# Conversions and transposes of the late weights tied behind the additions and products written ahead of them

## The chip, the cores and the metric

The kernel runs on one core of one Trainium2 chip. The metric is the device time of one execution in microseconds (us), the median of the runs that were made; lower is better. The core has a matrix engine (TensorE, "PE" in the profile, with its weight loads as "PEld"), three elementwise engines (VectorE "DVE", ScalarE "ACT", GpSimd "POOL"), and a queue engine (SyncE, "SP") that starts the DMA transfers here. Each engine runs its instructions strictly in the order of its own queue and waits on semaphores for the others.

## What is computed

Packed attention over 8 batches, then two feed-forward blocks. The part that matters is the second half of the first block and the weights of the second:

```python
x = np.ascontiguousarray(attn_out.transpose(0, 2, 1, 3)).reshape(B * S, H * D)   # 4608 x 512

def _moe_ref(x, w_gate, w_val, w_out):          # 512 -> 1536 -> 512
    g = x @ w_gate
    silu = g * (1.0 / (1.0 + np.exp(-g)))
    val = x @ w_val
    return (silu * val @ w_out).astype(np.float32)

def _moe2_ref(x, w1, w2, w3, w_out):            # 512 -> 1024 -> 1024 -> 512
    a = x @ w1
    b = x @ w2
    h = a * b @ w3
    return (h @ w_out).astype(np.float32)
```

`w3` and the second `w_out` have nothing between them, so the kernel multiplies them once (1024 x 1024 by 1024 x 512) and uses the product as one weight. The weights arrive as 64-bit numbers and must be turned into 32-bit ones on the chip. Every large product is made of three matmuls, high part by high part, high by low and low by high, so each operand is split into `hi` and `lo`.

## The kernel before

The tokens go through the first block in four passes P of two batches each (2P and 2P + 1, the first index in names such as `u6_2`), and in each pass over twelve blocks f of 128 columns (the second index). For every batch and block, stage 1 makes two products on PE, `pg` and `pv` (12 matmuls each, L445); ACT writes `u = Silu(pg)` (L450), DVE multiplies `u` by `pv` (L454), ACT rounds it to `uh` (L96) and POOL subtracts to get `ul` (L89). After every third block, stage 3 multiplies three blocks of `uh`, `ul` by the output weights into six tiles `px` (L674, 18 matmuls each, three tiles at a time); the first of the four groups of a pass is copied to `acc` by ACT (L682), the later ones are added to it by DVE (L686). Ahead of three blocks come their `pc` products (32 matmuls each, L412), which ACT and DVE split into `ch` and `cl`. PSUM is used as four tiles in turn: a new `pg`, `pv`, `px`, `pc` or `pw` must wait until the reader of the tile's last content is done.

During the last pass (P = 3, batches 6 and 7, blocks 0 to 9) `w3_task` is called at one to four places ("slots") of each block, and each call does a piece of the weight work of the second block. The list of pieces is four tiles of `w_out2`, eight of `w3`, and the same again (c = 0 and c = 1). For each tile, `w3_conv` converts it: ACT takes the high word (Prelu, L349), DVE shifts the low word (`vx`, L350) and joins the two (`vt`, L353); then the next raw tile is loaded. A `w_out2` tile is split on ACT and POOL (`wo2h`, `wo2l`). A `w3` tile (c, r) is transposed on DVE in the next call (`w3_T`, L749, one buffer), split on ACT (`w3h`) and POOL (`w3l`, two buffers each), and in the call after that multiplied: `pw` is 12 matmuls (L766) that take `w3h` first and `w3l` from the third matmul on. For c = 0 ACT copies the result out (L770); for c = 1 DVE adds the stored half to it (`w3o`, L772); either one frees the PSUM tile.

The order of each engine's queue is not written out: a scheduler sorts the instructions by their dependencies and by priority. `behind(x, what)` adds a dependency without a semaphore: it puts x behind the instruction `pin[what]` in the order and lets nothing wait for it at run time. Inside `w3_task` the dictionary `pin` was empty, so conversions and transposes went wherever the scheduler found their inputs ready. `pin_at` remembers the latest instruction of a kind as the program is written.

Of the kernel before, what the change touches and what calls it, by code (L numbers as in the profile page):

```python
# [13 lines left out]
ALU = mybir.AluOpType  # L14
# [24 lines left out]
def packed_attention_moe_kernel(  # L39
# [24 lines left out]
    nc = tc.nc  # L64
# [29 lines left out]
    def split(hi, lo, src, on="act", sub_on="dve"):  # L94
        if on == "act":
            nc.scalar.copy(hi, src)  # L96
        else:
            nc.vector.tensor_copy(hi, src)
        sub(lo, src, hi, sub_on)
# [26 lines left out]
    def psum(name):  # L126
        ps_n[0] += 1
        return ps_at[ps_n[0] % len(ps_at)].tile([128, 2, 512], F32, tag="A", name=name)
# [9 lines left out]
    in_front, conv_rest, pin, pin_at = [True], [], {}, {}  # L138
    NO_SYNC = mybir.DependencyInfo(mybir.DependencyClass.NoSync, mybir.DependencyReason.DATA)

    def behind(x, what):
        if what in pin:
            tc.add_manual_dep(x.ins, pin[what].ins.name, NO_SYNC, reason="behind the last unit")
# [192 lines left out]
    def conv(key, t):  # L336


        name, raw = raw_t.pop(0)
        assert name == key, (name, key)  # L340
        x = vc.tile(list(t.shape), I32, tag="vx", name=f"vx_{key}")
        w = raw.bitcast(I32)
        if len(t.shape) == 3:
            w = w.rearrange("p a (n e) -> p a n e", e=2)
            low, high = w[:, :, :, 0], w[:, :, :, 1]
        else:
            w = w.rearrange("p (n e) -> p n e", e=2)
            low, high = w[:, :, 0], w[:, :, 1]
        behind(nc.scalar.activation(t, high.bitcast(F32), AF.Prelu, scale=2.0 ** -112, alpha=-2.0 ** 32), "act")  # L349
        behind(nc.vector.tensor_scalar(x, low, 29, None, op0=ALU.logical_shift_right), "dve")  # L350

        def rest():
            nc.vector.scalar_tensor_tensor(  # L353
                t.bitcast(I32), t.bitcast(I32), 3, x, op0=ALU.logical_shift_left, op1=ALU.bitwise_or)

        if in_front[0]:
            conv_rest.append(rest)
        else:
            rest()
        if not in_front[0]:  # L360
            raw_load()
# [69 lines left out]
    def stage1(b, f, gv):  # L431
        if (b, f) not in s1_at:
            s1_at[b, f] = (up0 if in_front[0] or b % 2 == 0 else up).tile(
                [128, 2, HS], F32, tag="u", name=f"u{b}_{f}", bufs=1)
        u = s1_at[b, f]
        hi, lo = C_t[b // 2, f]
        ah, al = aT_t[b]
        cols = slice(128 * gv, 128 * gv + 128)
        t = psum(f"p{'gv'[gv]}{b}_{f}")
        for Q in range(2):  # L440
            for w, x, first, last in (
                (hi, ah, Q == 0, False), (hi, al, False, False), (lo, ah, False, Q == 1),
            ):
                for hf in range(2):
                    nc.tensor.matmul(  # L445
                        t[:, hf, 0:HS], lhsT=w[:, b % 2, Q, cols], rhs=x[:, Q, hf, :],
                        start=first, stop=last,
                    )
        if gv == 0:
            x = nc.scalar.activation(u, t[:, :, 0:HS], AF.Silu)  # L450
            if not in_front[0]:
                pin_at["act"] = x
            return
        x = nc.vector.tensor_tensor(out=u, in0=u, in1=t[:, :, 0:HS], op=ALU.mult)  # L454
        if not in_front[0]:
            pin_at["dve"] = x
        P = b // 2
        if (P, f) not in u_pair:
            at = up0 if len(u_pair) % NU < NU0 else up
            u_pair[P, f] = tuple(  # L460
                at.tile([128, 2, 2, HS], F32R, tag=f"u{x}", name=f"u{x}{P}_{f}") for x in "hl")
        uh, ul = u_pair[P, f]
        split(uh[:, b % 2], ul[:, b % 2], u, sub_on="pool")
        u_t[b, f] = (uh, ul)
# [53 lines left out]
    def pa_s(u):  # L518


        kT = kT_t.pop(u)
        t = psum(f"psp{u}")
        for hq in range(4):
            for e in range(2):
                es = slice(64 * e, 64 * e + 64)
                nc.tensor.matmul(
                    t[hs[hq], e, 0:HS].rearrange("j (m p) -> j m p", m=NR // 2), lhsT=kT[es, NR // 2, hs[hq]],
                    rhs=kT[es, 0:NR // 2, hs[hq]],
                    start=True, stop=True, tile_position=(64 * e, 32 * hq))
        mx = pa.tile([128, 1], F32, tag="mx", name=f"mx{u}")  # L530
        nc.vector.reduce_max(mx, t[:, :, 0:HS], axis=AX.XY)
        nc.vector.tensor_scalar_mul(mx, mx, -scale)
        return t, mx
# [77 lines left out]
    for f in range(2):  # L611
        task(CS[f] + 0.5, c_mm, 0, f)
        task(CO[f], lambda: c_out(*C_t["later"].pop(1)))
        for gv in range(2):
            task(S1[f] + gv, stage1, 0, f, gv)
# [7 lines left out]
    with tc.manual_schedule(engines=M0):  # L623
        for s in range(last + 1):
# [8 lines left out]
            if 0 <= s - 1 < U:  # L633
                x = pa_s(s - 1)
# [25 lines left out]
    acc = {}  # L660

    CW = 2 * S // 3
# [16 lines left out]
    def stage3_out(P, g, j, t):  # L679
        if g == 0:  # L680
            o = up.tile([128, 2, CW], F32, tag=f"acc{j}", name=f"acc{P}_{j}", bufs=1)
            nc.scalar.copy(o, t[:, :, 0:CW])  # L682
            acc[j] = o
        else:
            o = acc[j]
            pin_at["acc"] = nc.vector.tensor_tensor(out=o, in0=o, in1=t[:, :, 0:CW], op=ALU.add)  # L686
        if g == NG - 1:
            for h in range(2):
                d, c = divmod(2 * j + h, 3)
                t0 = 2 * S * P + CW * c  # L690
                if j % 3 == 1:
                    nc.sync.dma_start(X2d[d, :, t0:t0 + CW], o[:, h])
                elif h == 0:
                    nc.sync.dma_start(X2d[d, :, t0:t0 + 2 * CW], o.rearrange("p h s -> p (h s)"))

    def stage3(P, g, e):
        for j in range(ND // 2 * 3 // 2 * e, ND // 2 * 3 // 2 * (e + 1)):
            t = psum(f"px{P}_{g}_{j}")
            stage3_mm(P, g, j, t, range(GF))
            stage3_out(P, g, j, t)  # L700
# [31 lines left out]
    wo2_t, w3T = {}, {}  # L732

    def w3_conv(key):
        t = vl.tile([128, 512], F32, tag="vu", name=f"vt_{key}")
        conv(key, t)
        what, *at = key.split("_")
        c = int(at[0])
        if what == "wo2":
            hi = wp.tile([128, DM], F32R, tag="wo2h", name=f"wo2h{c}", bufs=W3B)  # L740
            lo = wp.tile([128, DM], F32R, tag="wo2l", name=f"wo2l{c}", bufs=W3B)
            split(hi, lo, t, sub_on="pool")
            wo2_t[c] = (hi, lo)
        else:
            w3T[c, int(at[1])] = t

    def w3_T(new):
        t = wp.tile([128, 512], F32, tag="w3T", name=f"w3T{new}", bufs=1)
        nc.vector.transpose(out=t, in_=w3T[new])  # L749
        hi = wp.tile([128, 4, 32, 4], F32R, tag="w3h", name=f"w3h{new}")  # L750
        lo = wp.tile([128, 4, 32, 4], F32R, tag="w3l", name=f"w3l{new}")
        split(hi, lo, t.rearrange("p (r k b) -> p k b r", r=4, k=4), sub_on="pool")
        w3T[new] = tuple(x.rearrange("p k b r -> p k (b r)") for x in (hi, lo))
# [21 lines left out]
    def w3_step(new, old):  # L775
        if old is not None:
            w3_mm(old)
        if new is not None:
            w3_T(new)
# [91 lines left out]
    def w3_task(P, f, slot):  # L871

        if P < NPR - 1 or slot not in W3S[f % GF] or f > 9 or (f == 0 and slot < 3):
            return
        i = w3_at[0]
        w3_at[0] += 1
        if 0 < i <= len(w3_list) and w3_list[i - 1].startswith("w3"):
            new = tuple(int(x) for x in w3_list[i - 1].split("_")[1:])
            w3_step(new, w3_old[0])
            w3_old[0] = new  # L880
            if new[1] == NF2 - 1:
                w3_step(None, new)
                w3_old[0] = None
        if i < len(w3_list):
            w3_conv(w3_list[i])

    for n, (P, f) in enumerate(steps):
        def at(i):
# [2 lines left out]
        if P > 0:  # L891
            wo_split(P, f)
        w3_task(P, f, 0)
        if n > 1 and at(1) is not None and n < NF:
            c_mm(*at(1))
# [5 lines left out]
        if (2 * P, f) not in u_t:  # L901
            stage1(2 * P, f, 0)
            stage1(2 * P, f, 1)
# [13 lines left out]
        if at(1) is not None and at(1)[0] > 0:  # L917
            wo_load(*at(1))
        w3_task(P, f, 1)
        if pend is not None:  # L920
            stage3(*pend, 0)
        w3_task(P, f, 2)
        stage1(2 * P + 1, f, 0)
        if n == 1:
# [210 lines left out]
```

## Time and profile before

| | us |
|---|---|
| median of three runs | 1360.7 (1360.44 to 1363.02) |
| the profiled execution | 1364.69 |
| its span in the trace | 1362.6 |
| PE busy in it | 1339.7 (98%) |
| DVE, ACT, POOL busy | 656.5, 570.1, 387.8 |

The span is what the trace records from first to last instruction; 2.1 us of the profiled execution lie around it. The mean granted clock of PE is 0.996. The weight work of `w3_task` lies between 580 and 785 us. The page cuts numbers out of names (`vt_w` stands for a `w3` tile, `vt_wo` for one of `w_out2`); only the `w3T`, `w3h` and `w3l` keep theirs.

### The profile page before, as it was taken

What the parts mean: (1) busy time and instruction counts of PE and PEld (TensorE: products, weight loads), DVE (VectorE), ACT (ScalarE), POOL (GpSimd) and SP (SyncE); (2) the same over time, 40 slices, a digit from 0 to 9 for tenths busy, and PEclk for the clock granted to TensorE, in tenths of its full rate; (3) what the DMA queues carried; (4) which work ended last, traced back from release to release, by engine and by line L of the source; (5) the groups of instructions that cost most, each with busy time, mean ns of one, the idle gap of its engine ahead of it and who ended that gap; (6) DMA issues with size and microseconds to landing.
All of it is one profiled execution on the core that took longest, in us unless ns stands there. A gap on an engine that the chain in (4) does not pass through costs nothing.

```text
span 1362.6 us, 25518 instructions
## 1 busy us (share of the span) xinstructions
PE 1339.7 (98%) x10196; PEld 1241.7 (91%) x10196; DVE 656.5 (48%) x962; ACT 570.1 (42%) x940; POOL 387.8 (28%) x309
## 2 busy tenths in 40 slices
PE   7999999999999999999999999999999999999998
PEld 5678899999999999989999999999899899998997
DVE  3756877336564466462463379633423234234230
ACT  5774644244443454344554146423333333233331
POOL 0332322323322333243444237312112021121120
PEclk9999999999999999989999999999999999999999
DMA  9976766534545443244443249828448266285441
GB/s 318 341 222 206 209 197 200 168 77 125 151 131 183 115 120 125 71 134 132 151 142 111 65 166 338 311 89 254 160 142 254 91 211 215 88 254 162 142 145 47
DMA packets 186822, 230.27 MB, mean 169 GB/s; under 512 B 70736, under 2 KB 117840, under 8 KB 186704
## 3 DMA queue, kind: packets, MB, share of 16 engines
q1 hardware_dynamic: 186704, 228.64, 53.7%
q8 instruction: 81, 1.33, 0.4%
q14 instruction: 37, 0.30, 0.1%
HBM read 179.04 MB, written 49.55 MB: 168 GB/s over the span
## 4 chain that ended last, share of the span: by engine, by line
PE 81%; DVE 4%; DMA 1%; issue 1%; ACT 1%; SPq 0%; POOL 0%; DVEq 0%; ACTq 0%
PE px L674 19%; PE po L1072 14%; PE pA L1008 13%; PE pg L445 9%; PE pv L445 9%; PE pB L1008 6%; PE pw L766 3%; PE pC L1008 3%; PE pc L412 2%; DVE ws L89 1%; PE psq L209 1%; DMA wo3r<-wo3d 0%; DMA x2r<-X2d 0%; DVE x2T L836 0%; DMA X2d<-acc 0%
## 5 line engine op out<-in xcount | busy, mean ns | idle before, releaser
L89 POOL TENSOR_TENSOR ul<-u,uh 128x576 fp32r<-128x576 f32 x96 | 146.9, 1532 | 304.9 <-ACT uh L96 278.9
L1028 POOL TENSOR_TENSOR c<-s,s 128x384 f32<-128x384 f32 x48 | 49.2, 1024 | 375.7 <-ACT s L1023 375.5
L674 PE MATMUL px<-uh,woh 128*128 128x384 f32 x576 | 148.2, 338 | 0.2
L674 PE MATMUL px<-ul,woh 128*128 128x384 f32 x576 | 146.7, 335 | 0.0
L674 PE MATMUL px<-uh,wol 128*128 128x384 f32 x576 | 146.6, 335 | 0.0
L1023 ACT COPY s<-pA 128x384 f32<-128x384 f32 x144 | 69.0, 479 | 178.6 <-PE pA L1008 172.2
L454 DVE TENSOR_TENSOR u<-u,pv 128x576 f32<-128x576 f32 x96 | 72.0, 751 | 139.8 <-PE pv L445 126.3
L1072 PE MATMUL po<-wo_hi,abl 128*128 128x512 f32 x288 | 112.2, 390 | 0.0
L1072 PE MATMUL po<-wo_lo,abh 128*128 128x512 f32 x288 | 112.2, 390 | 0.0
L1072 PE MATMUL po<-wo_hi,abh 128*128 128x512 f32 x288 | 112.1, 389 | 0.0
L96 ACT CAST uh<-u 128x576 fp32r<-128x576 f32 x96 | 64.6, 673 | 110.7 <-DVE u L454 110.5
L674 PEld LDWEIGHTS px<-uh,woh 128*128 128x128 f32 x576 | 103.0, 189 | 6.4 <-issue 2.9
L686 DVE TENSOR_TENSOR acc<-acc,px 128x768 f32<-128x768 f32 x72 | 68.0, 948 | 81.5 <-PE px L674 81.1
L674 PEld LDWEIGHTS px<-ul,woh 128*128 128x128 f32 x576 | 104.4, 188 | 0.0
L674 PEld LDWEIGHTS px<-uh,wol 128*128 128x128 f32 x576 | 104.3, 188 | 0.0
L89 POOL TENSOR_TENSOR wol<-wof,woh 128x512 fp32r<-128x512 f32 x48 | 65.2, 1370 | 126.9 <-ACT woh L96 121.8
L89 DVE TENSOR_TENSOR abl<-ab,abh 128x768 fp32r<-128x768 f32 x48 | 49.2, 1025 | 105.3 <-ACT abh L96 105.2
L450 ACT ACTIVATE u<-pg 128x576 f32<-128x576 f32 x96 | 62.4, 650 | 88.3 <-PE pg L445 81.7
L445 PE MATMUL pg<-aTh,ch 128*128 128x288 f32 x384 | 84.3, 301 | 1.2 <-DVE cl L89 0.7
L445 PE MATMUL pv<-aTh,ch 128*128 128x288 f32 x384 | 82.9, 297 | 0.9 <-DVE cl L89 0.6
L445 PE MATMUL pg<-aTh,cl 128*128 128x288 f32 x384 | 82.4, 296 | 0.5 <-DVE cl L89 0.5
L445 PE MATMUL pg<-aTl,ch 128*128 128x288 f32 x384 | 82.6, 297 | 0.0
(308 smaller groups left out, 3093.6 us busy)
## 6 DMA issues: line engine op xcount, KB each, us to landing
ws<-wsd SPq DMA_DIRECT2D x245, 256.0 KB, 3.0
wf<-Wd SPq DMA_DIRECT2D x36, 512.0 KB, 6.4
wsd<-ws SPq DMA_DIRECT2D x49, 256.0 KB, 3.6
km<-in_k_dram SPq DMA_DIRECT2D x16, 576.0 KB, 7.8
wof<-wod SPq DMA_DIRECT2D x36, 256.0 KB, 2.9
x2r<-X2d SPq DMA_DIRECT2D x24, 384.0 KB, 5.2
out_dram<-o SPq DMA_DIRECT2D x36, 256.0 KB, 2.0
vm<-in_v_dram SPq DMA_DIRECT2D x16, 512.0 KB, 8.2
```

Of the source, the lines that this page charges most:

```text
L89: x = eng.tensor_tensor(out=out, in0=src, in1=hi.bitcast(F32), op=ALU.subtract)
L96: nc.scalar.copy(hi, src)
L445: nc.tensor.matmul(t[:, hf, 0:HS], lhsT=w[:, b % 2, Q, cols], rhs=x[:, Q, hf, :], start=first, stop=last,)
L450: x = nc.scalar.activation(u, t[:, :, 0:HS], AF.Silu)
L454: x = nc.vector.tensor_tensor(out=u, in0=u, in1=t[:, :, 0:HS], op=ALU.mult)
L674: nc.tensor.matmul(t[:, h, 0:CW], lhsT=w[:, 128 * d:128 * d + 128], rhs=x[:, CW * c:CW * c + CW], start=first, stop=last,)
L686: pin_at["acc"] = nc.vector.tensor_tensor(out=o, in0=o, in1=t[:, :, 0:CW], op=ALU.add)
L766: nc.tensor.matmul(t[:, 1], lhsT=a[:, kk], rhs=w, start=(i == 0), stop=(i == 11))
L1008: nc.tensor.matmul(bk[n], lhsT=w[:, hl, 128 * d:128 * d + 128], rhs=r[:, d], start=(first and d == 0 and i == 0), stop=(d == 1 and i == 2) ...
L1023: nc.scalar.copy(o, t)
L1028: on.tensor_tensor(out=r, in0=o, in1=t, op=op)
L1072: nc.tensor.matmul(t, lhsT=a[:, j, cols], rhs=w[:, f], start=first, stop=last)
```

## The change

Two places remember one more instruction: stage 1 the product of L454, and stage 3 the addition of L686, both under the key "out", so that the later written one of the two stands there. `w3_task` fills `pin` before its work and empties it after: what goes through `behind(x, "dve")` is put behind the latest product or addition written so far, and what goes through `behind(x, "act")` behind the latest Silu. That holds for `vx` on DVE and the Prelu on ACT, which called `behind` already, and for the transposes of `w3`, which are now given to it as well. `vt` follows `vx` by its data, and the splits follow the transposes. No instruction is added or removed, and nothing is computed in another way.

```diff
@@ stage1
         x = nc.vector.tensor_tensor(out=u, in0=u, in1=t[:, :, 0:HS], op=ALU.mult)
         if not in_front[0]:
-            pin_at["dve"] = x
+            pin_at["dve"] = pin_at["out"] = x
@@ stage3_out
             o = acc[j]
-            pin_at["acc"] = nc.vector.tensor_tensor(out=o, in0=o, in1=t[:, :, 0:CW], op=ALU.add)
+            pin_at["acc"] = pin_at["out"] = nc.vector.tensor_tensor(out=o, in0=o, in1=t[:, :, 0:CW], op=ALU.add)
@@ w3_T
-        nc.vector.transpose(out=t, in_=w3T[new])
+        behind(nc.vector.transpose(out=t, in_=w3T[new]), "dve")
@@ w3_task
         w3_at[0] += 1
+        pin.update(dve=pin_at["out"], act=pin_at["act"])
         if 0 < i <= len(w3_list) and w3_list[i - 1].startswith("w3"):
...
         if i < len(w3_list):
             w3_conv(w3_list[i])
+        pin.clear()
```

Three places of DVE's queue show what moves. The order of PE's matmuls stays as it was, but for one `px` matmul that changes places with one of the first `pw`. The first place is the end of pass 2 and the first block of pass 3, where the last group of `px` of pass 2 is added to `acc2_0` to `acc2_2`. Before:

```order
L454 TENSOR_TENSOR u6_0_7013<-u6_0_7013,pv6_0_7028 128x576
L353 SCALAR_TENSOR_TENSOR vt_wo2_3_7432<-vt_wo2_3_7432,vx_wo2_3_7433 128x512
L350 TENSOR_SCALAR vx_w3_0_0_7478<-raw_w3_0_0_7282 128x512
L350 TENSOR_SCALAR vx_w3_0_1_7498<-raw_w3_0_1_7337 128x512
L353 SCALAR_TENSOR_TENSOR vt_w3_0_0_7477<-vt_w3_0_0_7477,vx_w3_0_0_7478 128x512
L749 STREAM_TRANSPOSE w3T(0, 0)_7491<-vt_w3_0_0_7477 128x512
L686 TENSOR_TENSOR acc2_0_5726<-acc2_0_5726,px2_3_0_7050 128x768
L353 SCALAR_TENSOR_TENSOR vt_w3_0_1_7497<-vt_w3_0_1_7497,vx_w3_0_1_7498 128x512
L749 STREAM_TRANSPOSE w3T(0, 1)_7560<-vt_w3_0_1_7497 128x512
L686 TENSOR_TENSOR acc2_1_5747<-acc2_1_5747,px2_3_1_7071 128x768
L350 TENSOR_SCALAR vx_w3_0_2_7567<-raw_w3_0_2_7382 128x512
L353 SCALAR_TENSOR_TENSOR vt_w3_0_2_7566<-vt_w3_0_2_7566,vx_w3_0_2_7567 128x512
L749 STREAM_TRANSPOSE w3T(0, 2)_7655<-vt_w3_0_2_7566 128x512
L686 TENSOR_TENSOR acc2_2_5768<-acc2_2_5768,px2_3_2_7093 128x768
L454 TENSOR_TENSOR u7_0_7114<-u7_0_7114,pv7_0_7129 128x576
```

and now:

```order
L454 TENSOR_TENSOR u6_0_7013<-u6_0_7013,pv6_0_7028 128x576
L686 TENSOR_TENSOR acc2_0_5726<-acc2_0_5726,px2_3_0_7050 128x768
L686 TENSOR_TENSOR acc2_1_5747<-acc2_1_5747,px2_3_1_7071 128x768
L686 TENSOR_TENSOR acc2_2_5768<-acc2_2_5768,px2_3_2_7093 128x768
L454 TENSOR_TENSOR u7_0_7114<-u7_0_7114,pv7_0_7129 128x576
L89 TENSOR_TENSOR cl3_1_7163<-pc3_1_7145,ch3_1_7162 128x1024
L89 TENSOR_TENSOR cl3_2_7184<-pc3_2_7166,ch3_2_7183 128x1024
L89 TENSOR_TENSOR cl3_3_7205<-pc3_3_7187,ch3_3_7204 128x1024
L686 TENSOR_TENSOR acc2_3_5909<-acc2_3_5909,px2_3_3_7208 128x768
```

The conversions and transposes of `w3` that stood among the three additions are gone from there, and the first of them now come after `acc2_5` and later products.

The second place is in blocks 2 and 3 of pass 3, just ahead of the first `pw`, which is `pw3_0_0`. Before:

```order
L454 TENSOR_TENSOR u6_2_7395<-u6_2_7395,pv6_2_7410 128x576
L350 TENSOR_SCALAR vx_w3_0_5_7924<-raw_w3_0_5_7502 128x512
L454 TENSOR_TENSOR u7_2_7446<-u7_2_7446,pv7_2_7461 128x576
L454 TENSOR_TENSOR u6_3_7507<-u6_3_7507,pv6_3_7522 128x576
L350 TENSOR_SCALAR vx_w3_0_6_7987<-raw_w3_0_6_7571 128x512
L749 STREAM_TRANSPOSE w3T(0, 3)_7844<-vt_w3_0_3_7661 128x512
L353 SCALAR_TENSOR_TENSOR vt_w3_0_5_7923<-vt_w3_0_5_7923,vx_w3_0_5_7924 128x512
```

and now:

```order
L353 SCALAR_TENSOR_TENSOR vt_wo2_3_7432<-vt_wo2_3_7432,vx_wo2_3_7433 128x512
L454 TENSOR_TENSOR u7_2_7446<-u7_2_7446,pv7_2_7461 128x576
L350 TENSOR_SCALAR vx_w3_0_0_7478<-raw_w3_0_0_7282 128x512
L353 SCALAR_TENSOR_TENSOR vt_w3_0_0_7477<-vt_w3_0_0_7477,vx_w3_0_0_7478 128x512
L749 STREAM_TRANSPOSE w3T(0, 0)_7491<-vt_w3_0_0_7477 128x512
L454 TENSOR_TENSOR u6_3_7507<-u6_3_7507,pv6_3_7522 128x576
L350 TENSOR_SCALAR vx_w3_0_1_7498<-raw_w3_0_1_7337 128x512
L353 SCALAR_TENSOR_TENSOR vt_w3_0_1_7497<-vt_w3_0_1_7497,vx_w3_0_1_7498 128x512
L749 STREAM_TRANSPOSE w3T(0, 1)_7560<-vt_w3_0_1_7497 128x512
```

The conversion and the transpose of the first `w3` tile, (0, 0), which were done one block earlier, now stand behind the product `u7_2`, and PE multiplies that tile right after the `pv` of `u6_3`.

The third place is in blocks 7 to 9, where the tiles (1, 0) to (1, 4) are multiplied and added. Before:

```order
L454 TENSOR_TENSOR u7_7_8516<-u7_7_8516,pv7_7_8531 128x576
L772 TENSOR_TENSOR w3o1_0_8562<-part0_8548,pw3_1_0_8547 128x512
L749 STREAM_TRANSPOSE w3T(1, 3)_8703<-vt_w3_1_3_8644 128x512
L353 SCALAR_TENSOR_TENSOR vt_w3_1_5_8742<-vt_w3_1_5_8742,vx_w3_1_5_8743 128x512
L454 TENSOR_TENSOR u6_8_8585<-u6_8_8585,pv6_8_8600 128x576
L350 TENSOR_SCALAR vx_w3_1_7_8896<-raw_w3_1_7_8649 128x512
L772 TENSOR_TENSOR w3o1_1_8635<-part1_8621,pw3_1_1_8620 128x512
L749 STREAM_TRANSPOSE w3T(1, 4)_8736<-vt_w3_1_4_8709 128x512
```

and now:

```order
L454 TENSOR_TENSOR u7_8_8654<-u7_8_8654,pv7_8_8669 128x576
L749 STREAM_TRANSPOSE w3T(1, 3)_8703<-vt_w3_1_3_8644 128x512
L350 TENSOR_SCALAR vx_w3_1_4_8710<-raw_w3_1_4_8454 128x512
L353 SCALAR_TENSOR_TENSOR vt_w3_1_4_8709<-vt_w3_1_4_8709,vx_w3_1_4_8710 128x512
L749 STREAM_TRANSPOSE w3T(1, 4)_8736<-vt_w3_1_4_8709 128x512
L350 TENSOR_SCALAR vx_w3_1_5_8743<-raw_w3_1_5_8511 128x512
L353 SCALAR_TENSOR_TENSOR vt_w3_1_5_8742<-vt_w3_1_5_8742,vx_w3_1_5_8743 128x512
L772 TENSOR_TENSOR w3o1_0_8562<-part0_8548,pw3_1_0_8547 128x512
L454 TENSOR_TENSOR u6_9_8747<-u6_9_8747,pv6_9_8762 128x576
```

The transpose of (1, 3) stands behind `u7_8` instead of ahead of `u6_8`, and the addition `w3o1_0`, which stood right behind `u7_7`, comes after the transpose of (1, 4) and the conversion of (1, 5). On ACT the Prelu of (1, 5), which `vt_w3_1_5` needs, stands behind the rounding of (1, 4). `pg6_9`, which PE runs after `pw3_1_3`, takes the PSUM tile that `w3o1_0` frees.

## Rows read from the trace of the kernel before

**Rows 1.** The page, part 1: busy time, share of the span, instructions of each engine.

```profile
PE 1339.7 (98%) x10196; PEld 1241.7 (91%) x10196; DVE 656.5 (48%) x962; ACT 570.1 (42%) x940; POOL 387.8 (28%) x309
```

**Rows 2.** What PE waited for from 440 to 830 us: total, times, longest.

```profile
PE pc L412 <- DVE acc L686: 2.9, 1, 2.9
...
```

**Rows 3.** Timeline of PE: start, us, what [idle before it <- what ended that].

```profile
599.22 3.67 PE L412 MATMUL pc<-wf,PTd 64*32 64x256 f32 x64 [2.94 <-DVE acc L686]
```

**Rows 4.** Timeline of DVE, 595 to 599 us.

```profile
595.98 1.53 DVE L353 SCALAR_TENSOR_TENSOR vt_w<-vt_w,vx_w 128x512 int32<-128x512 int32 x1 [0.66 <-ACT vt_w L349]
597.62 0.71 DVE L749 STREAM_TRANSPOSE w3T(0, 2)_7655<-vt_w 128x512 f32<-128x512 f32 x1
598.25 0.92 DVE L686 TENSOR_TENSOR acc<-acc,px 128x768 f32<-128x768 f32 x1
```

**Rows 5.** Engines in 1 us stretches: us, PE, PEld, DVE, ACT, POOL busy; PEclk; DMA.

```profile
598.00:599.00 1.00, 0.00 (x0) 0.00 (x0) 1.00 (x2) 0.00 (x0) 0.00 (x0) 0.65 0.02 6
599.00:600.00 1.00, 0.78 (x16) 0.45 (x24) 0.83 (x2) 0.14 (x1) 0.00 (x0) 0.50 0.00 0
605.00:606.00 1.00, 1.00 (x7) 1.00 (x6) 0.90 (x2) 1.00 (x2) 0.00 (x0) 0.93 0.81 295
...
85.00:86.00 1.00, 0.01 (x1) 0.04 (x1) 0.81 (x5) 1.00 (x3) 0.00 (x0) 1.00 0.32 70
86.00:87.00 1.00, 1.00 (x5) 0.75 (x5) 0.95 (x1) 0.28 (x2) 0.00 (x0) 0.65 0.75 291
```

**Rows 6.** The chain of work, 590 to 780 us: start, us, what.

```profile
602.89 10.62 PE px L674 x54
...
629.51 2.76 PE pw L766 x12
...
647.59 2.75 PE pc L412 x96
650.34 9.56 PE px L674 x54
...
683.72 5.49 PE pw L766 x24
...
735.56 5.49 PE pw L766 x24
741.05 1.59 PE pg L445 x12
```

**Rows 7.** The same chain ahead of the stall: splitting the tile (0, 0).

```profile
589.84 0.72 DVE w3T(0, 0)_7491 L749
...
590.59 1.15 ACT w3h(0, 0)_7493 L96
...
591.80 1.62 POOL w3l(0, 0)_7494 L89
...
595.26 0.70 ACT vt_w L349
```

**Rows 8.** Timelines of DVE, ACT and POOL, 614 to 640 and 757 to 785 us.

```profile
614.42 0.42 DVE L350 TENSOR_SCALAR vx_w<-raw_w 128x512 int32<-128x512 int32 x1
614.94 0.69 DVE L353 SCALAR_TENSOR_TENSOR vt_w<-vt_w,vx_w 128x512 int32<-128x512 int32 x1
626.41 0.75 DVE L454 TENSOR_TENSOR u<-u,pv 128x576 f32<-128x576 f32 x1 [2.11 <-PE pv L445]
628.00 0.65 ACT L450 ACTIVATE u<-pg 128x576 f32<-128x576 f32 x1
627.94 1.43 POOL L89 TENSOR_TENSOR ul<-u,uh 128x576 fp32r<-128x576 f32 x1 [1.77 <-ACT uh L96]
759.17 0.69 DVE L772 TENSOR_TENSOR w3o<-part,pw 128x512 f32<-128x512 f32 x1 [1.81 <-PE pw L766]
```

**Rows 9.** Timelines of DVE and POOL, 584 to 590 us.

```profile
588.03 1.78 DVE L353 SCALAR_TENSOR_TENSOR vt_w<-vt_w,vx_w 128x512 int32<-128x512 int32 x1
587.78 1.47 POOL L89 TENSOR_TENSOR wo2l<-vt_wo,wo2h 128x512 fp32r<-128x512 f32 x1
```

## The prediction

> **What bounds the kernel now.** I read the page's busy times first: PE is busy 98% of the span, the other engines half of it or less [rows 1]. So the time changes only by what PE waits, or by its clock. Next, what PE waited for between 440 and 830 us, where the weight work lies: one wait of 2.9 us, by `pc` for the addition to `acc`, stands at its head [rows 2]. In the timeline of PE that wait stands ahead of 64 matmuls at 599.22 [rows 3]; these are `pc3_2` and `pc3_3`. DVE shows the cause: ahead of the addition (598.25) it ends a conversion of `w3` and a transpose (595.98, 597.62) [rows 4], which the change takes from there. Last, the clock: PE's granted clock was 0.65 in the microsecond from 598, 0.50 from 599, and 0.93 in that from 605 [rows 5], so half speed, 1.2 of 2.4 GHz, for some seven microseconds, after PE had stood idle.
>
> **What it takes away.** The wait itself is 2.94 us [rows 3]. The 64 `pc` matmuls took 3.67, while 96 at full clock took 2.75, so 64 are 1.83: 1.84 lost. The 54 `px` behind them took 10.62 instead of 9.56: 1.06 lost [rows 3, 6]. Together 2.94 + 1.84 + 1.06 = **5.84 us**, of which 2.90 is the clock. After the change `acc2_2` follows `acc2_1` directly and its `px` is done before `pg7_0` begins, so I count all of it as won, and see nothing that becomes late in its place: the conversions of `w_out2` moved away are needed 30 us later.
>
> **What it adds.** No instruction, and no semaphore. But order is a wait in itself: a transpose that used to be done one block early now stands behind the product written just ahead of it, and the matmuls that take the tile come a few microseconds later on an engine with no slack. The chain behind a product is transpose 0.72, `w3h` 1.15, `w3l` 1.62 [rows 7]; POOL has an `ul` of 1.43 ahead of `w3l` [rows 8]. The `pw` of 12 matmuls takes 2.76 [rows 6], 0.23 each, so `w3l` is due 0.46 after its start.
>
> *First kind: PE waits for the tile.* `pw3_0_0`, due at 629.51 [rows 6]: `u7_2` starts at 626.41 and ends at 627.16 [rows 8]. Behind it stand `vx` and `vt` of (0, 0) (0.42 and 0.69 [rows 8]), then transpose, `w3h`, `w3l`, with Silu and `uh` beside them on ACT. Without any hindrance `w3h` begins at about 629.4 and `w3l` ends at about 632.2: PE waits 1.0 and then 1.25, so 2.25. But `ul` of `u7_2` runs from 627.94 to 629.37 on POOL, just when `vt` would start. In the trace a `vt` took 1.78 instead of 0.69 while a `wo2l` ran from 587.78 to 589.25: it ended 0.56 after POOL, so it ran only once POOL was done [rows 8, 9]. Then `vt` ends at 630.1, `w3h` near 632.4, `w3l` near 634.1: 4.1 us. If `wo2l` and a second lock come in the way, 5.8. I take 4.1, since the row of a locked `vt` is the case at hand.
>
> The Trainium skill (SBUF — State Buffer, section "Who interferes with whom") says that VectorE and GpSimd share one pair of ports, held by whoever issues first for the whole instruction, and that a VectorE operation with two inputs in SBUF needs it. That speaks against this change, which puts such operations right behind the `ul` of the same slot; the trace agrees with it at 588.03. With the rule the place costs 4.1 us, without it 2.25.
>
> `pw3_0_7`, which follows `pw3_0_6` at 683.72 + 2.75 = 686.47 [rows 6]: its transpose stands behind `u7_5` (ends at 684.6, by the distance of 0.1 from `pv` to product and 0.75 for it), so the transpose ends at 685.3, `w3h` at 686.5, `ul` at 686.7, `w3l` at 688.3, while it is due at 686.9: 1.4 to 1.85, I take 1.6. By the same working: `pw3_1_0` 1.05 to 1.8, take 1.5; `pw3_1_3`, behind `u7_8`, which follows the `pv` that ends at 735.56 [rows 6], 1.4 to 2.25, take 1.8; `pw3_1_7`, behind `acc3_5`, 1.2 to 1.5, take 1.3; one tile of `px3_0` waits for a `cl` behind a conversion, 0 to 0.9, take 0.4. Other `pw` have a half of stage 3 (9.4 us) ahead of them and lose nothing. First kind: 4.1 + 1.6 + 1.5 + 1.8 + 1.3 + 0.4 = **10.7 us**, from 7.3 to 14.1.
>
> *Second kind: PE waits for a PSUM tile.* `pw3_1_1` to `pw3_1_3` hold three of four tiles; `pg6_9`, at 741.05 in the trace [rows 6], needs the one that `w3o1_0` frees. Before, this addition was done as soon as its `pw` was. Now it stands on DVE behind the transpose of (1, 4), which waits for the end of `w3l` of (1, 3), and behind `vt` of (1, 5), whose Prelu stands on ACT behind `w3h` of (1, 4). From the end of that `w3l`: 0.72 + 1.15 + 0.70 (Prelu) + 0.69 (`vt`) + 0.69 (`w3o`) = 3.95 [rows 7, 8], up to 4.85 if `vt` is locked out by `w3l` of (1, 4). PE has 10 more matmuls of `pw3_1_3` to do from then, 2.3. So 1.55 to 2.5, take 2.3. With the other tiles still held, each user waits for the one before: `pv6_9` for the Silu of `pg6_9`, 0.65 + 0.1 [rows 8]; `pw3_1_4` for the product, 0.75 + 0.1. `px3_2_0` waits for `w3o1_1`, behind the transpose and conversion of (1, 5) and (1, 6) in the same way: 3.95 to 4.85 from the transpose's start against 2.76 of `pw3_1_4` [rows 6], so 1.2 to 2.35 with hand-overs, take 1.8. `px3_2_1` waits for the addition of `px3_2_0`, 0.92 [rows 4] and 0.1. Second kind: 2.3 + 0.75 + 0.9 + 1.8 + 1.05 = **6.8 us**, from 5.3 to 7.7.
>
> *Clock.* The trace has two idle stretches of PE with a lower clock behind them, the one of 2.94 us, and one around 85 to 86, where the clock fell to 0.65 in the next microsecond [rows 5]; in both small matmuls went ahead. A new wait may do that or not. One such spell cost 2.90 us above; I take 1.5, a half chance of one, and bound it by nothing and by two, 5.8. Later work moved by this (the loads of the next stage) I bound by 0 and 1.3 and take as nothing.
>
> **Sum.** -5.84 + 10.7 + 6.8 + 1.5 = +13.2 us. On the profiled execution, 1364.69 with its span of 1362.6, this is 1377.9; the median of the runs is 4.0 lower, and I give the time against that: 1360.7 + 13.2 = **1374**. All terms at their low ends give +6.8, 1367.5.
>
> **The rivals.**
>
> *The new waits are hidden* (the other side). The stall goes and the tiles are ready in time, if the new waits stay under 5.84 together, half a microsecond at each of eleven places. For it: the engines other than PE are half idle [rows 1], and if `w3l` had no `ul` ahead of it, four of the places would lose nearly all. Against it: the tile's chain from the product is 0.72 + 1.15 + 1.62 = 3.5 at least [rows 7], more than the time left at five places. It gives 1360.7 - 5.8 = 1354.9. Chance 0.06.
>
> *Only the tiles' waits hit.* DVE reaches the `w3o` early enough, because PE, held at `pw3_1_3`, gives it time. Then -5.84 + 10.7 = +4.9: 1365.6. For it: DVE is idle half of the time; against it: the queue order between the transpose and `w3o1_0` is fixed, and the transposes wait for the same `w3l`. Chance 0.19.
>
> *The clock falls more than once and the locks are long.* Upper ends: -5.84 + 14.1 + 7.7 + 5.8 = +21.8: 1382.5. For it: from 738 to 755 six waits follow one another. Against it: this needs all ends at once. Chance 0.17.
>
> *Gain and waits cancel.* Low ends and a chain that overlaps more than the rows say: within 2.7 us of 1360.7, the 0.2% that a measurement of this kernel can tell from no change. Chance 0.08. That nothing moves is excluded by the order of the two builds.
>
> **How the numbers follow.** The forecast, both kinds of waits with at most one spell of low clock, has 0.50: 1374, its own range 1368 to 1380. Slower by over 0.2%: 0.50 + 0.19 + 0.17 = 0.86; within: 0.08; faster: 0.06. For 8 in 10 the range takes the forecast, most of the second rival and the nearer part of the third: 1364 to 1382.
>
> **What would show it.** The wait of `pc` for `acc` gone at 596 and the clock at 1.00 there; in PE's waits `pw` for `w3h` and `w3l` with some 10 us, longest near 630; `pg` for `w3o` (L774 by then), `pw` for the product and `px` for `w3o` and `acc` together some 7 us, at 740 to 765; a second `vt` of 1.5 us or more near 629. Were PE to run through from 629 to 645 without a wait, I would be wrong in the main.

## The result, and the profile after

The changed kernel took 1377.96 us (median, 1376.88 to 1378.82) against 1360.57 for the kernel before: a ratio of 1.0124, 95% interval [1.0112, 1.0137], so 17.4 us slower, between 15 and 19 by the interval. The forecast was 1374, with a range of 1364 to 1382. Of the nine executions of the kernel before that stand beside the first four variants below, one took 4644.93 us: the ratios leave it out, and it moves their median, 1361.79, by less than 0.1.

The wait that stood at the head of the stretch before [rows 2] is gone. What PE waited for between 440 and 840 us in the changed kernel, in total, times, longest (only lines behind the edit in `w3_task` have moved, so `w3o` is still at L772, where the prediction looked for L774):

```profile
PE pw L766 <- ACT w3h(0, 0)_7493 L96: 2.0, 1, 2.0
PE px L674 <- DVE w3o L772: 1.8, 1, 1.8
PE pw L766 <- POOL w3l(1, 3)_8706 L89: 1.7, 1, 1.7
PE pw L766 <- POOL w3l(1, 0)_8503 L89: 1.4, 1, 1.4
PE pw L766 <- POOL w3l(0, 7)_8119 L89: 1.4, 1, 1.4
PE px L674 <- DVE acc L686: 1.0, 1, 1.0
PE pw L766 <- DVE u L454: 0.9, 1, 0.9
PE pw L766 <- POOL w3l(1, 7)_9054 L89: 0.9, 1, 0.9
PE pv L445 <- ACT u L450: 0.7, 1, 0.7
PE pw L766 <- POOL w3l(0, 0)_7494 L89: 0.7, 1, 0.7
PE pg L445 <- DVE w3o L772: 0.6, 1, 0.6
...
PE px L674 <- DVE cl L89: 0.3, 1, 0.3
```

One wait of 2.9 has become twelve of 0.3 to 2.0. The lines with `pw` and `w3h` or `w3l`, and the `cl`, are what the prediction called the first kind (8.4 us together); the lines with `w3o`, `acc`, `u` are the second kind (5.0). The clock is the other half of the picture. The changed kernel in 1 us stretches, columns as in [rows 5]:

```profile
626.00:627.00 1.00, 1.00 (x5) 0.74 (x4) 0.90 (x3) 0.10 (x1) 1.00 (x1) 0.54 0.68 210
627.00:628.00 1.00, 1.00 (x4) 0.81 (x3) 0.61 (x1) 1.00 (x1) 0.33 (x1) 0.50 0.65 174
628.00:629.00 1.00, 1.00 (x4) 0.81 (x3) 0.00 (x0) 0.03 (x1) 0.90 (x1) 0.50 0.40 125
629.00:630.00 1.00, 1.00 (x5) 0.83 (x5) 0.00 (x0) 0.27 (x1) 0.64 (x1) 0.75 0.00 0
...
742.00:743.00 1.00, 1.00 (x3) 0.81 (x4) 0.99 (x2) 0.23 (x1) 0.00 (x0) 0.57 0.00 0
743.00:744.00 1.00, 1.00 (x4) 0.81 (x3) 0.00 (x0) 1.00 (x2) 0.05 (x1) 0.50 0.00 0
744.00:745.00 1.00, 1.00 (x3) 0.76 (x3) 0.52 (x1) 0.45 (x1) 1.00 (x1) 0.50 0.00 0
745.00:746.00 1.00, 1.00 (x4) 0.56 (x2) 1.00 (x2) 0.00 (x0) 0.49 (x1) 0.73 0.00 0
```

The spell of half clock at 599 [rows 5] is gone, and two new ones stand behind the waits at 622 and 740. While PE was busy it lost 0.46 + 0.50 + 0.50 + 0.25 = 1.7 us in the first and 1.7 in the second.

Third, DVE. The joinings of the two words of `w3` tiles (`vt_w`) behind 600 us, in the kernel before and then in the changed one: count, then ns of one as min/median/max, then the first and last start.

```profile
L353 DVE SCALAR_TENSOR_TENSOR vt_w<-vt_w,vx_w x13: 682/693/1665, 605.5 to 743.7; 128x512 int32<-128x512 int32 x13
```

```profile
L353 DVE SCALAR_TENSOR_TENSOR vt_w<-vt_w,vx_w x16: 691/1667/1903, 620.4 to 769.9; 128x512 int32<-128x512 int32 x16
```

The same instruction takes 0.69 us in the one order and 1.67 in the other, in the median. It now comes right behind a product, when POOL is subtracting for `ul` or a weight.

### The profile page after: what moved, and what is told of

Its sections match the earlier page's. It is cut to its first block, busy times and chain, and to the rows that moved or that the text cites. A ratio compares the mean times of both kernels' runs of the same rounds, so it can differ in the third digit from the quotient of the medians.

```text
span 1376.3 us, 25526 instructions
## 1 busy us (share of the span) xinstructions
PE 1341.3 (97%) x10196; PEld 1239.7 (90%) x10196; DVE 668.4 (49%) x962; ACT 569.7 (41%) x940; POOL 390.7 (28%) x309
## 4 chain that ended last, share of the span: by engine, by line
PE 46%; DVE 3%; DMA 2%; POOL 1%; issue 1%; ACT 1%; SPq 1%; ACTq 0%; DVEq 0%; POOLq 0%
PE po L1074 14%; PE pA L1010 13%; PE pB L1010 7%; PE px L674 4%; PE pC L1010 3%; PE pw L766 2%; PE pg L445 1%; PE pv L445 1%; DMA wo3r<-wo3d 1%; DMA raw_w<-in_moe_w_dram 1%; SPq L331 1%; DVE vt_w L353 1%; POOL ul L89 0%; DMA wsd<-ws 0%; PE pc L412 0%
## 5 line engine op out<-in xcount | busy, mean ns | idle before, releaser
L454 DVE TENSOR_TENSOR u<-u,pv 128x576 f32<-128x576 f32 x96 | 72.0, 751 | 165.9 <-PE pv L445 152.0
L686 DVE TENSOR_TENSOR acc<-acc,px 128x768 f32<-128x768 f32 x72 | 68.3, 952 | 101.4 <-PE px L674 100.8
```

What stands on the lines that cost most here:

```text
L686: pin_at["acc"] = pin_at["out"] = nc.vector.tensor_tensor(out=o, in0=o, in1=t[:, :, 0:CW], op=ALU.add)
```

## The experiments

The prediction's theory is that PE waits in two ways, each from its own part of the change: for the tile, because the **transposes** stand behind the product of their own slot, and for PSUM, because the **conversions** come late and push `w3o` back. The gain is the stall at 596 and nothing else. The rivals are that any tying makes everything late, that both kinds of waits come from the transposes, and that the long `vt` has another cause than POOL.

### Only the two tasks that made the stall are tied

```diff
         w3_at[0] += 1
-        pin.update(dve=pin_at["out"], act=pin_at["act"])
+        if i == 0:
+            pin_at["first"] = pin_at["out"]
+        if i in (5, 6):
+            pin.update(dve=pin_at["first"])
```

> Only the tasks 5 and 6 (conversions of w3 (0,1) and (0,2), transposes of (0,0) and (0,1)) are tied, and to one fixed place, the last addition of pass 2; ACT and all other tasks are free as before. Theory (the gain is the stall alone, the loss comes from the other tied tasks): the wait of pc for acc at 596 and the half clock behind it are gone, no new wait of PE over 0.5 us between 600 and 800, so 5.9 us less than before: about 1354.7, ratio 0.9957. Rival (any tying makes the chain of w3 late, as the transposes of (0,0) to (0,2) now come 20 us later): pw3_0_0 waits for its tile and the gain shrinks to 2 us or less. Rival (the stall is won but the time comes back at the next stage's start): within 1 us of before.

Measured: 1356.49 against 1361.79 for the kernel before on the same chip, 5.3 us less by the medians; ratio 0.9967 [0.9954, 0.9980], which is between 2.7 and 6.3 us. Against the changed kernel, 17.4 us slower than before, that is some 22 us better. In this kernel the wait at 596 is gone, no wait of PE is left between 600 and 800 us, and the 96 `pc` matmuls run in one piece:

```profile
594.52 2.82 PE L412 MATMUL pc<-wf,PTd 64*32 64x256 f32 x96
```

The additions of pass 2 on DVE, which stood behind a transpose and a conversion each before [rows 4], come as their `px` are done:

```profile
587.63 1.81 DVE L686 TENSOR_TENSOR acc<-acc,px 128x768 f32<-128x768 f32 x2
591.43 0.95 DVE L686 TENSOR_TENSOR acc<-acc,px 128x768 f32<-128x768 f32 x1 [2.00 <-PE px L674]
```

The last addition starts at 591.4, three microseconds ahead of the `pc` that needs its tile. So the gain that the prediction counted is there to be had, and a tie does no harm by itself: the tiles (0, 0) to (0, 2) come some 20 us later than before and are still in time. Both rivals fall. The gain is one of the changed order at one place. The loss comes either from the other tied tasks or from the place that the tasks are tied to, which in the change is the latest product each time; this run changes both, and no run here ties all the tasks to one early place.

### Transposes tied, conversions free

```diff
-        behind(nc.vector.transpose(out=t, in_=w3T[new]), "dve")
+        behind(nc.vector.transpose(out=t, in_=w3T[new]), "out")
...
-        pin.update(dve=pin_at["out"], act=pin_at["act"])
+        pin.update(out=pin_at["out"])
```

> All transposes tied behind the latest product or addition, as in the change; conversions on ACT and DVE free as before. Theory of two kinds of waits (transposes behind the product of their own slot make PE wait for the tile; late conversions make w3o and with it the PSUM tiles late): the stall at 596 is gone (-5.9), pw waits for w3h and w3l at pw3_0_0, 0_7, 1_0, 1_3, 1_7 (about 1.0 + 1.9 + 1.7 + 1.8 + 1.5), but pg6_9, pv6_9, pw3_1_4 and px3_2 wait for no w3o, product or Silu: +2.3 in all, about 1363. Rival (both kinds come from the transposes): w3o waits stay, +8 and more, about 1369 to 1378.

Measured: 1370.37, ratio 1.0069 [1.0053, 1.0085], 8.6 us slower than before. The kinds came apart as the theory says: PE waits for tiles (9.0 us, with the `cl`) and not once for `w3o`, a product or a Silu. The size was missed by 6.3 us (8.6 instead of 2.3), and one place explains about half of it: `pw3_0_7` waits 3.5 us instead of 1.9, and the clock falls behind it (0.50 from 685 to 688), which costs another 1.5: its last ten matmuls take 3.8 us from 685.34 on, where ten at 0.23 take 2.3. Its timeline of PE, and of DVE ahead of it, in this kernel:

```profile
683.40 0.50 PE L766 MATMUL pw<-wo2h,w3h(0, 7)_8118 128*128 128x512 f32 x1 [2.33 <-ACT w3h(0, 7)_8118 L96]
685.34 0.80 PE L766 MATMUL pw<-wo2h,w3l(0, 7)_8119 128*128 128x512 f32 x1 [1.20 <-POOL w3l(0, 7)_8119 L89]
```

```profile
680.25 0.69 DVE L353 SCALAR_TENSOR_TENSOR vt_wo<-vt_wo,vx_wo 128x512 int32<-128x512 int32 x1 [2.29 <-ACT vt_wo L349]
680.86 0.75 DVE L454 TENSOR_TENSOR u<-u,pv 128x576 f32<-128x576 f32 x1
681.52 0.70 DVE L749 STREAM_TRANSPOSE w3T(0, 7)_8116<-vt_w 128x512 f32<-128x512 f32 x1
```

A conversion left free was sorted ahead of the product, and at run time DVE stood 2.29 us before it, waiting for a Prelu; product and transpose queued behind it. The rest fits a loss at each stop that no wait shows (below).

### The change in the first half alone, and in the second half alone

```diff
+        if i < NH + NF2:
             pin.update(dve=pin_at["out"], act=pin_at["act"])
```

> Tied as in the change, but only in the tasks of the first half (w_out2 and w3 for c = 0, tasks 0 to 11); the second half is free as before. In this build the transposes of (1, r) stand ahead of the product of their slot again, but the conversions come as late as in the change, as each waits for the buffers of the one before. Theory of two kinds: -5.9 for the stall, pw3_0_0 with its clock spell +5, no waits of pw for w3l at 1_0, 1_3, 1_7, but the waits of pg6_9, pv6_9, pw3_1_4, px3_2_0 and px3_2_1 as in the change, +6 to +8: in all +5 to +8, 1366 to 1368. Rival (the second kind comes from late transposes): none of them, about 1360.

Measured: 1368.76, ratio 1.0053 [1.0039, 1.0067], 7.0 us slower than before. In the second half of this kernel no `pw` waits for a tile, since the transposes are early again, and yet the second kind is there. The timeline of PE at that place, waits only:

```profile
739.50 0.53 PE L445 MATMUL pg<-aTh,ch 128*128 128x288 f32 x2 [1.13 <-DVE w3o L772]
742.08 0.53 PE L445 MATMUL pv<-aTh,ch 128*128 128x288 f32 x2 [0.74 <-ACT u L450]
744.85 0.50 PE L766 MATMUL pw<-wo2h,w3h(1, 4)_8738 128*128 128x512 f32 x1 [0.92 <-DVE u L454]
749.01 0.62 PE L674 MATMUL px<-uh,woh 128*128 128x384 f32 x2 [1.12 <-DVE w3o L772]
753.45 0.62 PE L674 MATMUL px<-uh,woh 128*128 128x384 f32 x2 [1.05 <-DVE acc L686]
```

Five waits, one behind the other, as each tile is passed on only when the last user is done. So the second kind needs no late transpose; late conversions are enough, and they stay late although nothing ties them any more here. With the tied transposes of the run before it was absent. Together the two runs settle which part makes which wait.

```diff
+        if i >= NH + NF2:
             pin.update(dve=pin_at["out"], act=pin_at["act"])
```

> Tied as in the change, but only in the tasks from 12 on (c = 1). Theory of two kinds: the stall at 596 and its clock stay, pw3_0_0 doesn't wait; pw waits for w3l at 0_7, 1_0, 1_3 and 1_7 (1.9 + 1.7 + 2 + 1.5), w3o is early enough for pg6_9: about +7, 1367.6. Rival (the second kind hangs on the tied tasks of c = 1 themselves): also w3o, Silu, product and px waits of 6 us, about 1374.

Measured: 1369.28, ratio 1.0062 [1.0048, 1.0076], 7.5 us slower than before. What PE waited for in this kernel, 440 to 840 us, down to 0.9:

```profile
PE pc L412 <- DVE acc L686: 2.9, 1, 2.9
PE pw L766 <- POOL w3l(1, 0)_8503 L89: 1.6, 1, 1.6
PE pw L766 <- POOL w3l(0, 7)_8119 L89: 1.4, 1, 1.4
PE pw L766 <- POOL w3l(1, 3)_8706 L89: 1.3, 1, 1.3
PE pw L766 <- POOL w3l(1, 7)_9054 L89: 0.9, 1, 0.9
```

The stall stays, four tiles come late, and no PSUM tile does: the conversions of the second half are tied, but the stream was early when it got there (the first `w3o` on DVE starts at 726.30, in the changed kernel at 745.96). The two halves together give 14.5 us, near the 17.4 of the whole.

### Only ACT tied, and only DVE tied

```diff
-        pin.update(dve=pin_at["out"], act=pin_at["act"])
+        pin.update(act=pin_at["act"])
```

> Only the Prelu on ACT is tied behind the latest Silu; vx and the transposes are free. DVE's order in this build has the transposes early for c = 1, but w3o_1_0 behind the conversion of (1,5), as in the change. Theory (whatever ties a conversion makes the whole stream late, as four raw buffers and two vt buffers chain the conversions; late conversions alone make the second kind of waits): stall at 596 gone (-5.5), pw3_0_0 waits 1 to 2 for its tile, no pw of c = 1 waits over 0.5, pg6_9, pv6_9, pw3_1_4, px3_2_0 and px3_2_1 wait 5 in all and cost 6 to 7: +2 to +4 against before, about 1364. Rival (the tie on DVE is what counts): like the kernel with two tied tasks, 1356, or like before.

Measured: 1365.37, ratio 1.0031 [1.0018, 1.0044], 4.4 us slower than before, a little over the 2 to 4 expected. PE waits for the first tile (1.4 and 1.5, more than the 1 to 2 expected in all, with the clock at 0.50 from 624 to 630 behind it) and then for Silu, product and addition around `pg6_9` (0.8, 0.9, 1.0); the two waits for `w3o` themselves, which were expected, don't appear, so three of the five links were there. The main point holds: with the tie on ACT alone, which ties no instruction of DVE, the stall goes and the stream still comes late.

```diff
-        pin.update(dve=pin_at["out"], act=pin_at["act"])
+        pin.update(dve=pin_at["out"])
```

> The change without its tie on ACT: vx and the transposes tied behind the latest product or addition, the Prelu free. DVE's order in this build is that of the change, row for row. Theory: the same waits of PE, within 2 of the changed kernel, 1377 to 1379. Rival (the Prelu behind the Silu holds the conversion up): w3o waits fall, since the Prelu of (1,5) no longer stands behind w3h of (1,4): 3 to 5 less, 1373 to 1375.

Measured: 1379.76 (1379.15 to 1381.12), ratio 1.0144 [1.0129, 1.0160], so 18.8 us slower than the kernel before on the same chip, where the change lost 17.4. The same places wait, with 3.8 instead of 2.0 for the first tile and 2.2 instead of 0.6 for `w3o`. At the first tile ACT stood 1.92 us in front of the free Prelu, until a `wo2l` was done (617.40). The tie on ACT adds nothing to the loss. The rival, that the Prelu behind `w3h` holds `w3o` up, is not settled by this run, because the free Prelu was sorted to the same place. ACT and DVE in this kernel:

```profile
742.62 1.13 ACT L96 CAST w3h(1, 4)_8738<-w3T(1, 4)_8736 128x512 fp32r<-128x512 f32 x1 [3.18 <-DVE w3T(1, 4)_8736 L749]
743.65 0.66 ACT L349 ACTIVATE vt_w<-raw_w 128x512 f32<-128x512 f32 x1
```

```profile
744.34 1.56 DVE L353 SCALAR_TENSOR_TENSOR vt_w<-vt_w,vx_w 128x512 int32<-128x512 int32 x1 [1.51 <-ACT vt_w L349]
```

DVE stands 1.51 us in front of the joining until that Prelu is done, and `w3o` follows the joining at 745.83. With its tie or without it, the Prelu behind `w3h` is a link of the chain, as the prediction had it.

### Is it POOL that stretches the joining?

```diff
-            lo = wp.tile([128, DM], F32R, tag="wo2l", name=f"wo2l{c}", bufs=W3B)
-            split(hi, lo, t, sub_on="pool")
-            wo2_t[c] = (hi, lo)
+            nc.scalar.copy(hi, t)
+            wo2_t[c] = (hi, hi)
```

> The change, with the low parts of w_out2 left out (the high part is used in their place): eight subtractions of 1.3 to 1.5 less on POOL, nothing else; DVE's order is that of the change. It asks whether POOL's work is what stretches the joining of the words (vt, 1.60 in the change just ahead of pw3_0_0 while a wo2l ran on POOL, 0.69 alone). Theory (DVE waits for POOL): vt of (0,0) takes 0.7 to 0.8, its transpose and w3h come 0.8 to 1.0 earlier, the wait of pw3_0_0 for w3h falls from 2.0 to 1.0 to 1.2; the waits of c = 1 stay. Rival (vt is long for its own data or for the Prelu): 1.6 and 2.0 as in the change.

Ahead of the first `pw`, POOL and DVE in the changed kernel:

```profile
619.96 1.48 POOL L89 TENSOR_TENSOR wo2l<-vt_wo,wo2h 128x512 fp32r<-128x512 f32 x1
```

```profile
619.49 0.80 DVE L350 TENSOR_SCALAR vx_w<-raw_w 128x512 int32<-128x512 int32 x1
620.39 1.60 DVE L353 SCALAR_TENSOR_TENSOR vt_w<-vt_w,vx_w 128x512 int32<-128x512 int32 x1
```

and DVE in the kernel without the low parts of `w_out2`:

```profile
619.36 0.42 DVE L350 TENSOR_SCALAR vx_w<-raw_w 128x512 int32<-128x512 int32 x1
619.88 0.69 DVE L353 SCALAR_TENSOR_TENSOR vt_w<-vt_w,vx_w 128x512 int32<-128x512 int32 x1
```

Measured: 1375.40 in one execution. With POOL's subtraction taken away the joining takes 0.69 us, the shift ahead of it 0.42, and the wait of the first `pw` for `w3h` falls from 2.0 to 0.7 us, more than expected. The waits of c = 1 stay (1.4, 1.7, 0.9). It is POOL, and not `wo2l` alone: of the sixteen joinings of the changed kernel, each of the eleven that took over 1.5 us began while a subtraction ran on POOL and ended 0.54 to 0.56 us behind the end of it (`ul`, `w3l` or `wo2l`), and the five of 0.69 began when none ran. The Trainium skill (SBUF — State Buffer, section "Who interferes with whom") describes this as a shared pair of ports that one of the two engines holds for the whole of an instruction, and the runs agree: in the changed kernel `wo2l` ended at 621.44 and the `vt` 0.55 us later.

### The kernel before, once more

Nothing is edited here; it is a second profile.

> The kernel before, profiled once more: which of its waits and clock spells come in every execution. Theory: the wait of 2.9 at 596 comes each time, as the order makes it; the lower clock behind it comes each time too, so that it costs 5.8 always. Rival: the clock falls in some executions only, and the stall costs 3 to 6.

Measured: 1361.94 in this execution. The wait came again with 2.95 us. The clock behind it did not do the same: it was at 0.50 for three whole microseconds instead of six, and the `px` ran at full speed. Two pieces of the chain of that execution:

```profile
596.78 3.65 PE pc L412 x64
600.43 9.56 PE px L674 x54
```

With the prediction's own working that is 2.95 + (3.65 - 1.83) = 4.8 us, not 5.8; in the kernel with only the second half tied the same stall cost 2.94 + 0.70 + 1.00 = 4.6. The wait is fixed by the order, the clock spell behind it differs from one execution to the next. Both theories were half right.

## Why the prediction held, point by point

From the first `pc` of pass 3 to the `pg` that follows `pw3_1_7`, the profiled execution before took 779.28 - 595.18 = 184.1 us, and the changed one 792.33 - 593.53 = 198.8. These are the two ends in the changed kernel, from the timeline and the chain:

```profile
593.53 2.82 PE L412 MATMUL pc<-wf,PTd 64*32 64x256 f32 x96
```

```profile
792.33 1.56 PE pg L445 x12
```

The loss there is 14.7 us. By terms:

| term | predicted | in the trace of after |
|---|---|---|
| stall and the clock behind it | -5.8 | -5.9 (to the place of `pw3_0_0`) |
| first kind: waits for the tile | 10.7 | 8.4 |
| second kind: waits for PSUM | 6.8 | 5.0 |
| half clock behind new waits | 1.5 | 3.4 |
| left over | 0 | 3.8 |

**The gain** was sized rightly for this pair of executions; in the two other profiles with the stall it is 4.8 and 4.6, and 5.3 (2.7 to 6.3) in the timed runs of the kernel that has it alone. Nothing else came late in the stall's place, as predicted.

**The first kind.** Every place that was named waits. Four are near the forecast: `pw3_0_7` 1.4 (1.6 predicted), `pw3_1_0` 1.4 (1.5), `pw3_1_3` 1.7 (1.8), the `cl` 0.3 (0.4). `pw3_1_7` came to 0.9 (1.3). `pw3_0_0` was put at 4.1 and waited 2.7: the locked `vt` was there, 1.60 instead of 0.69, but it was `wo2l`, not `ul` behind it, that held it, and that ended half a microsecond earlier than the `ul` would have; Silu and `uh` did not stand in the way either.

**The second kind.** The five waits stand one behind the other as predicted, and four of them agree to 0.1 us. `pg6_9` was put at 2.3 and waited 0.6. (The bounds beside the 2.3 were subtracted wrongly: 3.95 and 4.85 less 2.3 are 1.65 and 2.55, not 1.55 and 2.5. Neither the 2.3 nor the sum hangs on that.) The working itself was right but took PE at full speed: `pw3_1_3` ran at half clock just ahead of it and so used up the time. In the kernel without `wo2l`, where the clock stayed up at this place, the same wait is 2.2, so the second spell cost next to nothing of its own (1.7 lost and 0.6 waited, against 2.2):

```profile
743.77 0.53 PE L445 MATMUL pg<-aTh,ch 128*128 128x288 f32 x2 [2.16 <-DVE w3o L771]
```

What causes it was put too narrowly. The prediction named the transpose of (1, 4) and the conversion of (1, 5) as two steps of one chain; the runs show that the late conversions alone are enough (first half tied) and that the late transposes alone are not (transposes tied).

**The clock** was undersized: two spells of 1.7 us instead of half a chance of one of 2.9.

**What was missing.** The prediction put a stop at no more than its wait, without a reason. The 3.8 us left over are not in any wait and not in the clock, and spread over twelve stops they are 0.3 each. The timeline of PE at one of the stops shows where a part of it is:

```profile
684.58 0.40 PE L766 MATMUL pw<-wo2l,w3h(0, 7)_8118 128*128 128x512 f32 x1
686.34 0.50 PE L766 MATMUL pw<-wo2h,w3l(0, 7)_8119 128*128 128x512 f32 x1 [1.36 <-POOL w3l(0, 7)_8119 L89]
686.68 0.40 PE L766 MATMUL pw<-wo2h,w3h(0, 7)_8118 128*128 128x512 f32 x1
686.91 0.39 PE L766 MATMUL pw<-wo2l,w3h(0, 7)_8118 128*128 128x512 f32 x1
```

In a row these matmuls follow one another by 0.23 us although each lasts 0.40, so they overlap. The one that waited starts 1.76 after the one ahead of it, which is 1.53 late, while the idle time shown is 1.36; and the next follows by 0.34 instead of 0.23. This stop thus costs 0.28 more than the wait that is shown. Worked out in the same way from the starts of their matmuls, the eleven others cost 0.24 to 0.28 each, so the twelve make up about 3.2 of the 3.8. The remaining 0.6 is open.

**Where the two sums differ.** The forecast of +13.2 stands beside 14.7 in the stretch and 17.4 in the medians. The profiled execution of before was 4 us above its median (1364.69 against 1360.57), and the second one reached its first `pc` 2.4 us earlier (592.74 against 595.18) and took 1.1 us less for the same stretch, 775.74 - 592.74 = 183.0. Against that one the loss in the stretch is 15.8. The rest of 1.6 lies within the interval of the ratio.

**The rivals.** That the new waits are hidden fell with the first line of the waits. That only the tiles' waits hit describes the kernel with tied transposes, not this one. The upper case, with two clock spells, was right about the spells and wrong about the locks. The forecast's case held, with its waits too long (17.5 against 13.4) and its stops and clock too cheap (1.5 against 7.2), and that these errors nearly cancelled in the stretch was luck.

## What to carry to other kernels

Before tying work behind a latest instruction, ask at which of the places the order hurts, and tie that one to a fixed point: two tied tasks of 24 gained 5.3 us where tying all of them to the latest instruction lost 17.4. An ordering edge that nothing waits for at run time cost nothing in the first of these, but it takes away the lead with which side work runs ahead, and for an engine that is 98% busy a lost lead can become a stop, as it did at twelve places here. When you sum stops, add to each wait what the pipeline loses in stopping, some 0.25 us here, and leave room for a lower clock behind some of them.

## What the runs showed of the hardware

The lower clock does not follow from the length of the wait alone. In the changed kernel it fell at 742 behind a wait of 1.7 us; in the kernel without `wo2l`, at the same place of the program, waits of 1.7 and 2.2 us followed one another within seven microseconds and the clock stayed at 1.00. The microseconds in which PE started again behind each:

```profile
739.00:740.00 1.00, 0.95 (x4) 0.82 (x5) 0.97 (x2) 0.17 (x1) 0.00 (x0) 1.00 0.00 0
...
744.00:745.00 1.00, 1.00 (x9) 1.00 (x9) 0.00 (x0) 0.00 (x0) 0.00 (x0) 1.00 0.44 166
```

In the kernel with only DVE tied it stayed at half speed for some ten microseconds from 748 on, and the same stall of 2.9 us at 596 brought half speed for some 6.8, 3.4 and 3.4 us in three executions (the two profiles of the kernel before, and the kernel with the second half tied). What decides it is left open; no run here was made to tell it.

That a VectorE instruction of 0.69 us takes 1.6 to 1.9 when GpSimd is subtracting was known from one row before; that it happens to most of them (eleven of sixteen, with a median of 1.67 over all) once they are tied behind products was not expected in that measure. It works the other way too: in the changed kernel the seven `w3l` that began while a `vt_w` was in progress took 1.96 to 2.01 us, and eight others 1.54 to 1.57.
